# Streaming the feed-forward products' columns from the last to the first

## The chip, the cores and the metric

The kernel runs on one core of one Trainium2 chip. The metric is the device time of one execution in microseconds (us); the kernel before has a median of 1002.88 us over three runs (997.54, 1002.88 and 1003.29). The core's engines are TensorE (PE: matrix products, with PEld for the loads of the stationary operand), VectorE (DVE), ScalarE (ACT), GpSimd (POOL) and SyncE (SP), which issues the transfers here.

## The reference

Attention of two kinds over q, k and v of shape (4, 8, 576, 64): one over means of 4 neighbouring positions (144 of them), repeated 4 times afterwards, and one over a band of less than 4 positions around each query; the two results are added. The sum, as a matrix x of 2304 tokens by 512, goes through two feed-forwards:

```
h = x @ w_in                       # 512 x 2048
x = (h - tanh(h)) @ w_out          # 2048 x 512
gate = sigmoid(x @ w_gate)         # 512 x 1536
out  = (gate * (x @ w_val)) @ w_out2   # 1536 x 512
```

## The kernel before

The tokens are cut into 6 chunks of 384 (`N`), and everything of the feed-forwards is held transposed: 128 features on the partitions, 384 tokens in the free dimension. Each 32-bit number is split into a high part in the format fp32r and a rest (`split`, line 222: ScalarE copies, VectorE subtracts), and each product of two such numbers is made of three matmuls, high by high, high by rest and rest by high. `mm3` (lines 228 to 231) is the one place where they are issued. Its arguments are the output in PSUM, the two parts of the stationary operand, and the two parts of the moving operand.

A matmul has one stationary operand, 128 by 128, which a LDWEIGHTS row loads, and one moving operand, whose columns stream through the array one after the other; each gives one column of the output. There are three callers:

- `h_part` (line 533, called by `h_mm`): hidden features of a chunk. Stationary are the weights, moving is x, 384 columns; four parts of 128 input features accumulate in one bank of PSUM (`ab`). Used by the first feed-forward, and for gate and value of the second.
- `do_y` (line 576): the first feed-forward's second product. Moving is g, 384 columns; 16 blocks of hidden features accumulate in four banks (`acc`).
- `do_out` (line 734): the second feed-forward's second product. Here g is stationary and the weights move, 512 columns; 12 blocks accumulate in three banks at a time (`acc` and `ab`).

The order of the work is written out by hand: the engines' streams are in program order from the second chunk on, and the attention's small products are put between those of the feed-forwards by a counter (`tick`, `work`). The attention's own matmuls (lines 305 to 440) don't go through `mm3`. The results in PSUM are read by ScalarE and VectorE (tanh, sigmoid, copies), which wait by semaphores for the last of the matmuls that write a bank; a framework derives those waits from the tiles and regions that an instruction reads and writes.

Of the kernel before, what the change touches and what calls it, by code (L numbers as in the profile page):

```python
# [53 lines left out]
def tile_kernel(ctx: ExitStack, tc: tile.TileContext, qk, vp, v, w1, w2, mask, ident, out):  # L54
# [3 lines left out]
    def pool(name, bufs, stack=ctx, **kw):  # L58
        return stack.enter_context(tc.tile_pool(name=name, bufs=bufs, **kw))
# [8 lines left out]
    ap = pool("ap", 1, p1)  # L68
# [153 lines left out]
    def split(dst, src):  # L222
# [2 lines left out]
            out=dst[:, 1, :], in0=src, in1=dst[:, 0, :].bitcast(F32), op=ALU.subtract  # L225
        )

    def mm3(o, wh, wl, xh, xl, first, last):
        nc.tensor.matmul(out=o, lhsT=wh, rhs=xh, start=first, stop=False)  # L229
        nc.tensor.matmul(out=o, lhsT=wh, rhs=xl, start=False, stop=False)  # L230
        nc.tensor.matmul(out=o, lhsT=wl, rhs=xh, start=False, stop=last)  # L231
# [304 lines left out]
    def h_part(w, key, bank, k):  # L536
        wh, wl = (w[:, i, k * 128:(k + 1) * 128] for i in range(2))
        x = xt[key, k]
        mm3(bank[:, :N], wh, wl, x[:, 0, :], x[:, 1, :], k == 0, k == KD - 1)
# [34 lines left out]
    def do_y(c, f):  # L574
        g, w = gs.pop((c, f)), weight(1, f, 1)
        if f == 0:
            acc[c] = [acc_bank(e) for e in range(KD)]
        for e in range(KD):
            wh, wl = (w[:, i, e * 128:(e + 1) * 128] for i in range(2))
            mm3(acc[c][e][:, :N], wh, wl, g[:, 0, :], g[:, 1, :], f == 0, f == F1 - 1)  # L580
            if f == F1 - 1:
                defer(1, y_out, c, e)
            if e == 1:
                tick()
        y_done.add((c, f))
        tick()
# [150 lines left out]
    def do_out(i, f, s, g):  # L737
# [3 lines left out]
        for t, bank in enumerate(banks[s]):  # L741
            gh, gl = (g[:, x, t * 128:(t + 1) * 128] for x in range(2))
            mm3(bank, gh, gl, w[:, 0, :], w[:, 1, :], f == 0, f == F2 - 1)
            if f == F2 - 1:
                row = PAIRS[i][s] * N + t * 128
                last = i == len(PAIRS) - 1
                if last:

                    if not ends:
                        ends.extend(p.tile([128, WU], I64, tag="raw", name="ends").bitcast(F32) for p in (rawp, wpools["raw2"]))  # L750
                    at = 3 * s + t
                    o = ends[at // 4][:, at % 4 * DM:at % 4 * DM + DM]
                else:
                    o = xs2.tile([128, DM], F32, tag="o", name="o")
                if last and s == 1 and t == 2:
                    half = DM // 2
                    nc.vector.tensor_copy(out=o[:, :half], in_=bank[:, :half])
                    copy(o[:, half:], bank[:, half:])
                    store(out[row:row + 128, :half], o[:, :half])
                    store(out[row:row + 128, half:], o[:, half:])  # L760
                    continue
                if t % 2:
                    copy(o, bank)
                else:
                    nc.vector.tensor_copy(out=o, in_=bank)
                store(out[row:row + 128, :], o)
            if t == 1:
                tick()
# [91 lines left out]
```

## Time and profile before

| | |
|---|---|
| median of three runs | 1002.88 us (997.54 to 1003.29) |
| span of the profiled execution | 998.4 us; no other time of this execution is listed |
| PE busy | 979.2 us, 98% |
| PEld busy | 914.6 us, 92% |
| VectorE, ScalarE, GpSimd busy | 42%, 37%, 8% |
| share of PE in the chain that ended last | 91% |

The span runs from the first instruction to the last. Matmuls overlap their neighbours, so the mean duration of one is longer than the time it costs; what one costs is the distance from its start to the start of the next.

### The profile page before, as it was taken

How to read it: one execution, taken by the hardware profiler on the slowest of the kernel's cores; microseconds unless marked ns; L12 is line 12 of the kernel's file. 1: busy time of each engine (PE TensorE's matmuls, PEld its weight loads, DVE VectorE, ACT ScalarE, POOL GpSimd, SP SyncE). 2: the span in 40 equal slices, each digit the busy share in tenths (PEclk: the TensorE clock that was granted, in tenths of full speed). 3: DMA queues.
4: the chain of work that ended last, by engine and by line, in shares of the span. 5: the costliest groups of instructions: out<-in, count | busy, mean ns of one | idle time of the engine just before them, and what ended most of it. 6: DMA issues, size and time to landing. Idle time of an engine off the chain costs nothing.

```text
span 998.4 us, 15616 instructions
## 1 busy us (share of the span) xinstructions
PE 979.2 (98%) x6476; PEld 914.6 (92%) x6476; DVE 419.2 (42%) x736; ACT 372.2 (37%) x952; POOL 78.5 (8%) x89
## 2 busy tenths in 40 slices
PE   7889999999999999999999999999999999999998
PEld 7678889999999889999999999999999999999997
DVE  6898864334334343435666553113211114211112
ACT  5867754344344444434456342113111113111111
POOL 2153220300300320000000000000000000000000
PEclk9899999999999999999999999999999999999999
DMA  8566532212203211104444330002000002000001
GB/s 281 165 216 230 177 113 84 62 40 86 61 9 116 63 61 55 60 1 166 159 142 143 127 127 1 9 16 72 32 1 1 3 22 72 32 1 1 1 1 64
DMA packets 33256, 76.63 MB, mean 77 GB/s; under 512 B 3280, under 2 KB 23456, under 8 KB 28832
## 3 DMA queue, kind: packets, MB, share of 16 engines
q1 hardware_dynamic: 33184, 75.62, 23.0%
q8 instruction: 51, 0.84, 0.3%
q14 instruction: 21, 0.17, 0.1%
HBM read 63.02 MB, written 12.58 MB: 76 GB/s over the span
## 4 chain that ended last, share of the span: by engine, by line
PE 91%; DVE 3%; POOL 2%; DMA 2%; ACT 2%; issue 1%; SPq 0%; POOLq 0%; DVEq 0%; ACTq 0%
PE ab L229 18%; PE ab L231 18%; PE ab L230 18%; PE acc L229 10%; PE acc L230 9%; PE acc L231 9%; PE ab L440 2%; PE ab L372 2%; PE ab L305 1%; PE ab L432 1%; PE ab L346 1%; PE ab L334 1%; DMA qk<-in_qk 1%; DVE w L193 1%; PE acc L653 1%
## 5 line engine op out<-in xcount | busy, mean ns | idle before, releaser
L229 PE MATMUL ab<-x,w 128*128 128x384 f32 x952 | 325.5, 342 | 0.3 <-DVE t L242 0.3
L231 PE MATMUL ab<-x,w 128*128 128x384 f32 x952 | 320.4, 337 | 0.0
L230 PE MATMUL ab<-x,w 128*128 128x384 f32 x952 | 320.1, 336 | 0.0
L229 PEld LDWEIGHTS ab<-x,w 128*128 128x128 f32 x952 | 179.2, 188 | 7.6 <-issue 1.8
L230 PEld LDWEIGHTS ab<-x,w 128*128 128x128 f32 x952 | 179.4, 188 | 3.4
L231 PEld LDWEIGHTS ab<-x,w 128*128 128x128 f32 x952 | 179.2, 188 | 0.0
L785 DVE TENSOR_TENSOR p<-ab,p 128x384 f32<-128x384 f32 x72 | 40.2, 558 | 273.4 <-PE ab L231 273.4
L229 PE MATMUL acc<-g,w 128*128 128x384 f32 x384 | 133.2, 349 | 0.0
L230 PE MATMUL acc<-g,w 128*128 128x384 f32 x384 | 129.7, 338 | 0.0
L231 PE MATMUL acc<-g,w 128*128 128x384 f32 x384 | 129.1, 336 | 0.0
L242 DVE TENSOR_TENSOR t<-ab,t 128x384 f32<-128x384 f32 x94 | 52.3, 556 | 153.4 <-ACT t L554 153.4
L781 ACT ACTIVATE p<-ab 128x384 f32<-128x384 f32 x72 | 35.4, 491 | 183.4 <-PE ab L231 183.4
L554 ACT ACTIVATE t<-ab 128x384 f32<-128x384 f32 x94 | 45.9, 488 | 146.3 <-PE ab L231 130.5
L239 ACT ACTIVATE g<-p 128x384 fp32r<-128x384 f32 x72 | 37.8, 524 | 158.0 <-DVE p L785 158.0
L229 PEld LDWEIGHTS acc<-g,w 128*128 128x128 f32 x384 | 72.1, 188 | 2.4 <-issue 1.8
L230 PEld LDWEIGHTS acc<-g,w 128*128 128x128 f32 x384 | 72.3, 188 | 0.7 <-issue 0.6
L231 PEld LDWEIGHTS acc<-g,w 128*128 128x128 f32 x384 | 72.2, 188 | 0.0
L242 DVE TENSOR_TENSOR g<-t,g 128x384 fp32r<-128x384 f32 x96 | 55.9, 583 | 36.6 <-ACT g L239 35.4
L239 ACT ACTIVATE g<-t 128x384 fp32r<-128x384 f32 x96 | 50.3, 524 | 44.7 <-DVE t L242 44.7
L224 DVE TENSOR_TENSOR g<-p,g 128x384 fp32r<-128x384 f32 x72 | 40.2, 559 | 42.6 <-ACT g L239 42.6
L231 PE MATMUL acc<-w,g 128*128 128x512 f32 x144 | 57.1, 396 | 0.0
L230 PE MATMUL acc<-w,g 128*128 128x512 f32 x144 | 57.0, 396 | 0.0
(101 smaller groups left out, 1099.5 us busy)
## 6 DMA issues: line engine op xcount, KB each, us to landing
raw<-in_w SPq DMA_DIRECT2D x34, 1024.0 KB
qk<-in_qk SPq DMA_DIRECT2D x16, 576.0 KB
vr<-in_vp SPq DMA_DIRECT2D x16, 288.0 KB
x<-xo SPq DMA_DIRECT2D x20, 192.0 KB
xs<-x SPq DMA_DIRECT2D x20, 192.0 KB
y<-y SPq DMA_DIRECT2D x20, 192.0 KB
xs<-y SPq DMA_DIRECT2D x20, 192.0 KB
out<-o SPq DMA_DIRECT2D x12, 256.0 KB
```

The costliest lines, as they stand in the source:

```text
L193: nc.vector.tensor_tensor(out=t[:, 1, :], in0=w32, in1=t[:, 0, :].bitcast(F32), op=ALU.subtract)
L224: nc.vector.tensor_tensor(out=dst[:, 1, :], in0=src, in1=dst[:, 0, :].bitcast(F32), op=ALU.subtract)
L229: nc.tensor.matmul(out=o, lhsT=wh, rhs=xh, start=first, stop=False)
L230: nc.tensor.matmul(out=o, lhsT=wh, rhs=xl, start=False, stop=False)
L231: nc.tensor.matmul(out=o, lhsT=wl, rhs=xh, start=False, stop=last)
L239: nc.scalar.activation(out=dst, in_=src, func=ACTF.Copy)
L242: nc.vector.tensor_tensor(out=dst, in0=a, in1=b, op=ALU.subtract)
L372: nc.tensor.matmul(out=sb[r0:r0 + 64, x, :], lhsT=t[r0:r0 + 64, 0, QB * j:QB * j + QB], rhs=t[r0:r0 + 64, 1, w0:w0 + WIN], start=True, sto ...
L440: nc.tensor.matmul(out=ob[r0:r0 + 64, QB * x:QB * x + QB], lhsT=vw[0][:, j - n, i, r0:r0 + 64], rhs=pt[:, x, r0:r0 + 64], start=True, stop ...
L554: nc.scalar.activation(out=t, in_=hb[:, :N], func=ACTF.Tanh)
L781: nc.scalar.activation(out=p, in_=gate[:, :N], func=ACTF.Sigmoid)
L785: nc.vector.tensor_tensor(out=p, in0=val[:, :N], in1=p, op=ALU.mult)
```

## The change

The three matmuls get their output and their moving operand as access patterns that start at the last column and go down by one element. Column j of the input still ends in column j of the output; only the order in which the columns pass is turned. The stationary operand is as before. All calls of `mm3` are affected, no other matmul is.

```
+    def backwards(a):
+        step, n = a.ap[-1]
+        return bass.AP(tensor=a.tensor, offset=a.offset + step * (n - 1), ap=[list(a.ap[0]), [-step, n]])
+
     def mm3(o, wh, wl, xh, xl, first, last):
+        o, xh, xl = backwards(o), backwards(xh), backwards(xl)
         nc.tensor.matmul(out=o, lhsT=wh, rhs=xh, start=first, stop=False)
         nc.tensor.matmul(out=o, lhsT=wh, rhs=xl, start=False, stop=False)
         nc.tensor.matmul(out=o, lhsT=wl, rhs=xh, start=False, stop=last)
```

No instruction is added, removed or moved on any engine: the sequences of PE, VectorE, ScalarE, GpSimd and SyncE are the same but for the line numbers, which grow by 5 behind the new function. What differs is which semaphores some instructions wait for. The rows on PE that name PE's own semaphore grow from 88 to 143; those on VectorE that name PE's shrink from 203 to 146; ScalarE, GpSimd and SyncE wait as before.

On PE, in the second chunk of the first feed-forward, at the change from `do_y` (bank `acc_679`) to the next `do_h` (bank `ab_1845`, the third block of weights). Before:

```order
L229 MATMUL acc_679<-g_1730,w_1693 128x384
L230 MATMUL acc_679<-g_1730,w_1693 128x384
L231 MATMUL acc_679<-g_1730,w_1693 128x384
L229 MATMUL ab_1845<-x_1700,w_591 128x384
L230 MATMUL ab_1845<-x_1700,w_591 128x384
L231 MATMUL ab_1845<-x_1700,w_591 128x384
```

The same place with the change:

```order
L234 MATMUL acc_679<-g_1730,w_1693 128x384
L235 MATMUL acc_679<-g_1730,w_1693 128x384
L236 MATMUL acc_679<-g_1730,w_1693 128x384
L234 MATMUL ab_1845<-x_1700,w_591 128x384 [waits PE_49]
L235 MATMUL ab_1845<-x_1700,w_591 128x384
L236 MATMUL ab_1845<-x_1700,w_591 128x384
```

The first matmul into the bank now names PE's own semaphore; the order is untouched.

On VectorE, in the stretch of the first chunk in which the attention's products alternate with the feed-forward's; `g<-t,g` writes the rest of g behind ScalarE's copy of its high part. Before:

```order
L242 TENSOR_TENSOR t<-ab,t 128x384 [waits Activation_49]
L176 TENSOR_SCALAR raw<-raw 128x1024 [waits DMAHW2_49]
L178 SCALAR_TENSOR_TENSOR raw<-raw 128x1024 [waits DVE_49,Activation_49]
L242 TENSOR_TENSOR g<-t,g 128x384 [waits PE_49,Activation_49]
L416 SCALAR_TENSOR_TENSOR pl<-ab,mask_sb 128x420 [waits PE_49]
```

With the change:

```order
L247 TENSOR_TENSOR t<-ab,t 128x384 [waits Activation_49]
L176 TENSOR_SCALAR raw<-raw 128x1024 [waits DMAHW2_49]
L178 SCALAR_TENSOR_TENSOR raw<-raw 128x1024 [waits DVE_49,Activation_49]
L247 TENSOR_TENSOR g<-t,g 128x384 [waits Activation_49]
L421 SCALAR_TENSOR_TENSOR pl<-ab,mask_sb 128x420 [waits PE_49]
```

The subtraction no longer names PE beside ScalarE; it stands where it stood.

## Rows read from the trace of the kernel before

**Rows 1.** The page: the span, and busy time of each engine.

```profile
span 998.4 us, 15616 instructions
PE 979.2 (98%) x6476; PEld 914.6 (92%) x6476; DVE 419.2 (42%) x736; ACT 372.2 (37%) x952; POOL 78.5 (8%) x89
```

**Rows 2.** The page: the chain that ended last, by engine and by line.

```profile
PE 91%; DVE 3%; POOL 2%; DMA 2%; ACT 2%; issue 1%; SPq 0%; POOLq 0%; DVEq 0%; ACTq 0%
PE ab L229 18%; PE ab L231 18%; PE ab L230 18%; PE acc L229 10%; PE acc L230 9%; PE acc L231 9%; PE ab L440 2%; PE ab L372 2%; PE ab L305 1%; PE ab L432 1%; PE ab L346 1%; PE ab L334 1%; DMA qk<-in_qk 1%; DVE w L193 1%; PE acc L653 1%
```

**Rows 3.** Windows: stretch, length, busy PE, PEld, DVE, ACT, POOL; clock; DMA; GB/s.

```profile
75.00:80.00 5.00, 5.00 (x25) 4.74 (x24) 3.06 (x6) 2.04 (x5) 0.00 (x0) 0.70 0.68 216
400.00:600.00 200.00, 200.00 (x1203) 195.11 (x1203) 108.69 (x164) 93.08 (x166) 0.00 (x0) 1.00 0.33 115
600.00:800.00 200.00, 200.00 (x1056) 187.07 (x1055) 46.08 (x80) 39.08 (x77) 0.00 (x0) 1.00 0.05 17
800.00:990.00 190.00, 190.00 (x1004) 177.78 (x1003) 40.06 (x73) 35.08 (x71) 0.00 (x0) 1.00 0.05 16
```

**Rows 4.** Groups of PE, line 229: shapes, count, busy, mean ns, idle before.

```profile
L229 PE MATMUL ab<-x,w 128*128 128x384 f32 x952 | 325.5, 342 | 0.3 <-DVE t L242 0.3
...
L229 PE MATMUL acc<-g,w 128*128 128x384 f32 x384 | 133.2, 349 | 0.0
...
L229 PE MATMUL acc<-w,g 128*128 128x512 f32 x144 | 56.4, 392 | 0.0
L229 PE MATMUL ab<-w,g 128*128 128x512 f32 x72 | 28.5, 395 | 0.0
...
L229 PE MATMUL acc<-x,w 128*128 128x384 f32 x8 | 3.0, 439 | 0.0
```

**Rows 5.** Timeline of PE, second feed-forward: start us, duration us, instruction.

```profile
801.59 0.39 PE L229 MATMUL acc<-w,g 128*128 128x512 f32 x1
...
803.69 0.34 PE L229 MATMUL ab<-x,w 128*128 128x384 f32 x1
803.86 0.34 PE L230 MATMUL ab<-x,w 128*128 128x384 f32 x1
...
807.85 0.39 PE L229 MATMUL acc<-w,g 128*128 128x512 f32 x1
```

**Rows 6.** Timeline of PE at the low clock, first chunk.

```profile
75.48 0.52 PE L230 MATMUL ab<-x,w 128*128 128x384 f32 x1
75.80 0.52 PE L231 MATMUL ab<-x,w 128*128 128x384 f32 x1
...
76.76 0.52 PE L231 MATMUL ab<-x,w 128*128 128x384 f32 x1
```

**Rows 7.** Groups of PEld, line 229, gate, value and hidden features.

```profile
L229 PEld LDWEIGHTS ab<-x,w 128*128 128x128 f32 x952 | 179.2, 188 | 7.6 <-issue 1.8 <-DVE t L242 0.6 <-DVE ss L291 0.2
```

**Rows 8.** Groups of VectorE: same operations, adjacent elements and every second word.

```profile
L193 DVE TENSOR_TENSOR w<-raw,w 128x1024 fp32r<-128x1024 f32 x34 | 44.0, 1293 | 6.1 <-ACT w L239 6.1
...
L224 DVE TENSOR_TENSOR x<-xs,x 128x384 fp32r<-128x384 f32 x44 | 23.0, 554 | 6.8 <-ACT x L239 6.6
...
L594 DVE COPY y<-acc 128x384 f32<-128x384 f32 x10 | 5.5, 550 | 0.0
...
L765 DVE COPY o<-acc 128x512 f32<-128x512 f32 x6 | 4.1, 688 | 5.5 <-DMA out<-o 5.5
```

**Rows 9.** Timeline of PE: into banks ab_1845 (152.81) and ab_1967 (163.94).

```profile
152.63 0.34 PE L231 MATMUL acc<-g,w 128*128 128x384 f32 x1
152.81 0.34 PE L229 MATMUL ab<-x,w 128*128 128x384 f32 x1
...
163.76 0.34 PE L231 MATMUL acc<-g,w 128*128 128x384 f32 x1
163.94 0.34 PE L229 MATMUL ab<-x,w 128*128 128x384 f32 x1
```

## The prediction

> **What bounds the kernel now.** I read the page's busy times first: PE is busy 979.2 of 998.4 us, VectorE 42%, ScalarE 37% [rows 1]. A busy share alone says little of an engine whose instructions overlap, so the chain of waits came next. It runs over PE for 91% of the span, and the six entries of the three lines of `mm3` make up 82% of it (18, 18, 18, 10, 9 and 9) [rows 2]. The windows then say where that holds: from 400 to 990 us PE has no idle time and the clock is granted in full, while VectorE and ScalarE are busy for half of the time at most (108.69 and 93.08 of 200 us, later 46.08 and 39.08) [rows 3]. So the kernel ends when PE is through its stream, and the price of one matmul of `mm3` decides.
>
> That price is a distance between starts, not the mean of 342 ns in the groups [rows 4]. From the timeline: nine matmuls of 512 columns lie between 801.59 and 803.69, (803.69 - 801.59)/9 = 233.3 ns each; twenty-four of 384 columns lie between 803.69 and 807.85, 4.16/24 = 173.3 ns each [rows 5]. The counts for one of the three lines are 952 + 384 + 8 = 1344 of 384 columns and 144 + 72 = 216 of 512 [rows 4], so 4032 and 648 for all three. 4032 x 0.1733 = 698.9 us and 648 x 0.2333 = 151.2 us, together 850.1 us: 85% of the span goes through the three lines that are changed.
>
> [...]
>
> **The change, part by part.**
>
> *The columns' order.* 4680 matmuls read the moving operand downwards and write the bank downwards. The number of columns, the stationary operand and its loads stay. No row of the trace before shows an access in descending order, so its price is bounded. [...] From above: a column takes two clocks in place of one, the price that the low clock shows, 320 ns for 384 columns and 512/384 x 320 = 426.7 ns for 512 [rows 6]; that is 4032 x 146.7 ns + 648 x 193.3 ns = 591 + 125 = +717 us. Between these ends I take 0, by the nearest rows of another engine that walks memory out of simple order. VectorE subtracts 384 neighbouring elements in 554 ns and 1024 elements of which one input lies in every second word in 1293 ns; that is (1293 - 554)/640 = 1.15 ns per element, against (688 - 550)/128 = 1.08 ns for its copies of neighbouring elements [rows 8]. A step of two words costs there 7% at most. A step of minus one keeps neighbours closer than that: each address is beside the last one, and the set of words is the same as before. It is another engine and another direction, hence the wide bounds.
>
> *The new waits on PE.* 55 more rows on PE name PE's own semaphore. The wait is for work that PE has issued long before, or nothing would be known to be free; but if one had to wait until the matmul before it was out of the array, it would cost the difference of length and distance, 340 - 173 = 167 ns, 55 x 0.167 = 9.2 us in all. The trace has one to look at: the first matmul into `ab_1967` names that semaphore already before the change, and it starts 0.18 us after its predecessor (163.76 to 163.94). The first into `ab_1845` has no such wait before the change, and starts 0.18 us after its own (152.63 to 152.81) [rows 9]. I take 0, and keep 9.2 us as the upper end.
>
> *The waits that VectorE loses.* 57 rows of VectorE no longer name PE. They still wait for ScalarE's copy into the same tile, and VectorE isn't what PE waits for after 400 us [rows 3]. An earlier subtraction gains nothing there. In the first 100 us, where PE does idle, it may shift by fractions of a microsecond. I take 0. If the cover went (PE ahead of VectorE), each subtraction would count with its 0.55 us, but PE would have to become much faster for that.
>
> *Everything else.* ScalarE, GpSimd, SyncE and its transfers have the same instructions, order and waits. The semaphore behind a bank's last matmul comes when its last column is written, whichever column that is, so the readers are released as late as before.
>
> The sum is 998.4 + 0 + 0 + 0 = 998.4 us against the profiled execution's span, which is 4.5 us under the median of 1002.88 and inside the runs' 997.54 to 1003.29. Against the median I forecast **1003 us**: no change.
>
> **The rivals.**
>
> *Two clocks per column (slower).* The bank's write port, or the port that reads the moving operand, handles neighbouring words together only while the addresses rise. Descending columns would then go through one by one, at half the rate. [...] It lies at every one of the 4680 matmuls, each on the path, and costs 717 us in the full case: 1720 us. It decides against my forecast as soon as a matmul of 384 columns costs more than 175.4 ns, for 1% of the time is 10 us, and 10 of the 850 us is 1.2% of 173.3 ns. Against it: pairs of words that lie together upwards lie together downwards too (both lengths are even and the tiles begin with column 0), and VectorE's steps of two words cost little [rows 8]. [...] I give 0.16.
>
> *The excess doubles.* [...] 66.7 us more: 1070 us. [...] 0.10, which stands for all small prices up to that.
>
> *The excess goes (faster).* [...] 0.04.
>
> *The new waits drain the array.* 1012 us, at the edge of 1%. 0.03.
>
> *The pattern is turned back.* Output and input are turned together, so a compiler could write both upwards without changing a result. Nothing would then be different on the chip; this gives 1003 us as well, and I count it with my forecast.
>
> **How the numbers follow.** The forecast, 1003 us, has 0.67; by itself it lies between 993 and 1012 us (the runs' spread of 0.6%, and up to 9.2 us for the waits). With the waits that drain (0.03) and the doubled excess (0.10) the cases from 992 to 1072 us hold 0.80; left out are the half rate (0.16) and the lost excess (0.04). One per cent, 10 us, is what runs of this kernel can tell from no change. Faster by more: 0.04 and 0.01 of the forecast's lower edge, 0.05. Slower by more: 0.16 + 0.10 and half of the drained waits, 0.27. Within: 0.68.
>
> **What would show it.** Right: in the stretch from 400 us on, matmuls of 384 columns still start every 173 ns and those of 512 every 233 ns at the full clock, LDWEIGHTS stays at 188 ns, PE's first matmuls into a bank still follow after 0.17 to 0.18 us, and VectorE's idle time is still put down to PE. Two clocks per column would show as 320 and 427 ns at a granted clock of 1.00, with the span past 1700 us and every other engine's busy time unchanged. [...] Drained waits would show as gaps of up to 0.17 us at the 55 places with all other distances kept. My forecast fails if the distance moves at all in the undisturbed stretch; it would be wrong in its reasoning, though right in its number, if distance and waits moved against each other.

## The result and the profile after

| | before | changed |
|---|---|---|
| median | 1000.71 us, four runs | 1013.75 us, four runs |
| ratio | | 1.0123, 95% interval 1.0096 to 1.0149 |
| profiled execution | span 998.4 us | 1016.59 us, span 1014.8 us |

The changed kernel is slower by 1.2%, 12.3 us of 1000.71 (9.6 to 14.9). The time lies inside the range, but it isn't the forecast of no change: one term of the sum was taken as 0 and is about 13 us.

The page of the changed kernel, span and busy times, answers to [rows 1]:

```profile
span 1014.8 us, 15574 instructions
PE 995.1 (98%) x6476; PEld 929.1 (92%) x6476; DVE 417.5 (41%) x736; ACT 375.7 (37%) x952; POOL 78.2 (8%) x89
```

PE is busy 15.9 us longer, in a span that is 16.4 us longer; VectorE, ScalarE and GpSimd do what they did. The windows show it where PE never waits (stretch, length, busy PE with the number of matmuls, PEld, VectorE, ScalarE, GpSimd, granted clock, DMA share, GB/s); compare [rows 3]:

```profile
600.00:800.00 200.00, 200.00 (x1041) 186.83 (x1040) 49.14 (x83) 41.86 (x78) 0.00 (x0) 1.00 0.07 23
```

At the full clock 1041 matmuls fit into the 200 us that held 1056. The timeline of PE in the second feed-forward (start, duration) says which of them are dearer; it answers to [rows 5]:

```profile
802.84 0.40 PE L234 MATMUL acc<-w,g 128*128 128x512 f32 x1
...
804.94 0.34 PE L234 MATMUL ab<-x,w 128*128 128x384 f32 x1
805.11 0.34 PE L235 MATMUL ab<-x,w 128*128 128x384 f32 x1
805.29 0.34 PE L236 MATMUL ab<-x,w 128*128 128x384 f32 x1
805.46 0.34 PE L234 MATMUL ab<-x,w 128*128 128x384 f32 x1
...
809.18 0.40 PE L234 MATMUL acc<-w,g 128*128 128x512 f32 x1
```

Nine matmuls of 512 columns take 804.94 - 802.84 = 2.10 us, 233.3 ns each, as before. Twenty-four of 384 columns take 4.24 us in place of 4.16: 176.7 ns each in place of 173.3. The single starts lie 0.17 and 0.18 us apart in turn: one matmul has the old distance, the next is some 6.7 ns late. 4032 x 3.33 ns = 13.4 us. Over all matmuls of the rows `ab<-x,w` that start between 600 and 990 us, the mean distance is 176.6 ns against 173.6 before, 3.1 ns more, which makes 12.4 us; the 512-column ones there have 233.7 ns against 232.8, 0.6 us for all 648.

The loads of the stationary operand, which the change leaves alone, take 189 ns against 188 [rows 7]:

```profile
L234 PEld LDWEIGHTS ab<-x,w 128*128 128x128 f32 x952 | 179.6, 189 | 7.7 <-issue 2.0 <-DVE t L247 0.4 <-DVE xo L460 0.2
```

And the first matmul into `ab_1845`, which now names PE's own semaphore, follows as closely as before [rows 9], 0.18 us:

```profile
156.66 0.34 PE L236 MATMUL acc<-g,w 128*128 128x384 f32 x1
156.84 0.34 PE L234 MATMUL ab<-x,w 128*128 128x384 f32 x1
```

The stream accounts for some 13 of the profiled pair's 16.4 us. The other 3 us or so are near what the clock took in that execution. Two windows of the changed kernel:

```profile
30.00:47.00 17.00, 14.21 (x118) 10.34 (x113) 11.48 (x22) 13.56 (x47) 3.05 (x3) 0.70 0.46 151
...
329.00:337.00 8.00, 6.48 (x57) 5.69 (x57) 1.38 (x3) 1.28 (x3) 4.33 (x6) 0.79 0.02 8
```

The same two of the kernel before:

```profile
30.00:47.00 17.00, 14.34 (x135) 10.89 (x134) 13.17 (x25) 15.04 (x50) 2.54 (x3) 0.80 0.51 164
...
329.00:337.00 8.00, 8.00 (x69) 7.02 (x68) 3.80 (x10) 3.65 (x13) 1.81 (x2) 1.00 0.67 186
```

The granted clock is lower by 0.10 over 17 us and by 0.21 over 8 us, 1.7 + 1.7 = 3.4 us of full clock. PE's wait of 1.5 us in the second window doesn't count: the kernel before has it too, 1.8 us long and some 6 us earlier. The other three runs of the changed kernel had mean clocks of 0.992 to 0.997 against 0.990 here, and two of them are at 1009.97 and 1011.8 us; so this part comes and goes between executions.

### The profile page after: what moved, and what is told of

Read it like the earlier page. It is cut to its first block, busy times and chain, and to the rows that moved or that the text cites. A ratio compares the mean times of both kernels' runs of the same rounds, so it can differ in the third digit from the quotient of the medians.

```text
span 1014.8 us, 15574 instructions
## 1 busy us (share of the span) xinstructions
PE 995.1 (98%) x6476; PEld 929.1 (92%) x6476; DVE 417.5 (41%) x736; ACT 375.7 (37%) x952; POOL 78.2 (8%) x89
## 4 chain that ended last, share of the span: by engine, by line
PE 91%; DVE 3%; DMA 2%; ACT 2%; POOL 2%; issue 1%; SPq 0%; POOLq 0%; DVEq 0%; ACTq 0%
PE ab L234 18%; PE ab L235 18%; PE ab L236 18%; PE acc L234 10%; PE acc L235 9%; PE acc L236 9%; PE ab L377 2%; PE ab L445 2%; PE ab L310 1%; PE ab L437 1%; DMA qk<-in_qk 1%; PE ab L351 1%; PE ab L339 1%; PE acc L658 1%; DVE w L193 1%; ACT pl L429 1%
## 5 line engine op out<-in xcount | busy, mean ns | idle before, releaser
L234 PE MATMUL ab<-x,w 128*128 128x384 f32 x952 | 329.7, 346 | 0.1
L235 PE MATMUL ab<-x,w 128*128 128x384 f32 x952 | 324.6, 341 | 0.0
L236 PE MATMUL ab<-x,w 128*128 128x384 f32 x952 | 324.5, 341 | 0.0
L234 PE MATMUL acc<-g,w 128*128 128x384 f32 x384 | 134.5, 352 | 0.0
L235 PE MATMUL acc<-g,w 128*128 128x384 f32 x384 | 131.1, 341 | 0.0
L236 PE MATMUL acc<-g,w 128*128 128x384 f32 x384 | 130.4, 340 | 0.0
```

## Experiments

Theories at the outset: **R**, reading the moving operand downwards costs it; **W**, writing the bank downwards costs it; **S**, the 55 additional waits on PE cost it. Later **D**, the direction by itself, against **P**, the places of the two operands in memory.

**Reading alone.** `mm3` without the reversed output:

```
-        o, xh, xl = backwards(o), backwards(xh), backwards(xl)
+        xh, xl = backwards(xh), backwards(xl)
```

> Only the moving operand is read downwards; the results are written upwards, so that the products come out with their columns in reverse (inside each chunk of 384 tokens, and inside each row of the output). In the changed kernel the starts of 384-column matmuls lie 173.3 and 180.0 ns apart in turn, against 173.3 throughout before; 512 columns stay at 233.3 ns. Theory R (reading downwards costs it): 173.3 and 180.0 in turn again, about 4032/2 x 6.7 ns = 13.4 us, time near 1013 us. Theory W (writing downwards costs it): 173.3 ns throughout, time near 1001 us. Theory S (the 55 additional semaphore waits cost it): this kernel has the 88 waits of before, so 1001 us too, with 173.3 ns.

Measured: 1011.84 us, ratio 1.0097 (1.0071 to 1.0124). Timeline, a step of the second feed-forward:

```profile
805.24 0.40 PE L234 MATMUL acc<-w,g 128*128 128x512 f32 x1
807.34 0.34 PE L234 MATMUL ab<-x,w 128*128 128x384 f32 x1
...
811.58 0.40 PE L234 MATMUL acc<-w,g 128*128 128x512 f32 x1
```

4.24/24 = 176.7 ns for 384 columns, 2.10/9 = 233.3 ns for 512: the distances of the changed kernel, with the waits of the kernel before. R holds. By time it is 9.7 us by the ratio (7.1 to 12.4) and 11.0 us by the medians (1011.84 and 1000.87), somewhat less than the 13 us of the distances. Part of that is the clock: at a mean clock of 0.993 this kernel took 1012.66 and 1012.58 us, the kernel before 1000.54 us, 12.1 us apart. PE waits in the first 100 us for others, and a dearer matmul there may cost nothing, but that was not measured by itself.

**Writing alone.**

```
-        o, xh, xl = backwards(o), backwards(xh), backwards(xl)
+        o = backwards(o)
```

> Only the output in PSUM is written downwards, the moving operand is read upwards; columns come out in reverse. Theory R: 173.3 ns for 384 columns, time near 1001 us. Theory W: 173.3 and 180.0 ns in turn, near 1013 us. Theory S: this kernel has the 143 waits of the changed one, so about 1010 to 1013 us while the distances in the undisturbed stretch stay at 173.3 ns. If reading and writing cost only together (or only against each other), both this and the run with reading alone deviate from R and W in the same way.

Measured: 1001.55 us, ratio 1.0002 (0.9984 to 1.0019).

```profile
802.64 0.39 PE L234 MATMUL acc<-w,g 128*128 128x512 f32 x1
804.74 0.34 PE L234 MATMUL ab<-x,w 128*128 128x384 f32 x1
...
808.90 0.39 PE L234 MATMUL acc<-w,g 128*128 128x512 f32 x1
```

4.16/24 = 173.3 ns: as before. W falls by the distance, and S by the time, since this kernel has the changed kernel's 143 rows with PE's own semaphore (and VectorE's lost waits).

**Only the 512-column matmuls turned.**

```
+        if o.ap[-1][1] != N:
+            o, xh, xl = backwards(o), backwards(xh), backwards(xl)
```

> Reading and writing downwards for the 512-column matmuls alone (648 of 4680); same results as before. R and W both expect 233.3 ns as in the changed kernel and 173.3 ns for 384 columns, time as before, 998 to 1003 us. If the half pause of the 384-column matmuls is something that spreads from the stretch as a whole (a state that reading downwards leaves behind), the 384-column distances show 173.3 and 180.0 in turn here too.

Measured, one run: 999.78 us.

```profile
807.00 0.40 PE L235 MATMUL acc<-w,g 128*128 128x512 f32 x1
809.10 0.34 PE L235 MATMUL ab<-x,w 128*128 128x384 f32 x1
...
813.27 0.40 PE L235 MATMUL acc<-w,g 128*128 128x512 f32 x1
```

2.10/9 = 233.3 ns and 4.17/24 = 173.8 ns. Nothing is left behind for the 384-column matmuls; the whole cost is in those that are turned themselves, and the 512-column ones have next to none here (233.6 ns in mean between 600 and 990 us, 232.8 before).

**Matmuls alone.** 24 in a row of each kind, nothing else running:

```
    for n, rd, wr, cols, kind, at, step in CASES:
        ...
        for i in range(24):
            b = banks[i // 6][:cols, :]
            nc.tensor.matmul(
                out=pattern(b, *way(wr[i % len(wr)], n, at[1], step[1]), n),
                lhsT=w[:, 128 * (i % 4):128 * (i % 4) + cols],
                rhs=pattern(m, *way(rd[i % len(rd)], n, at[0], step[0]), n), start=(i % 6 == 0), stop=(i % 6 == 5),
            )
```

> Matmuls alone, none of the reference's work: 24 in a row of each kind, numbers of columns, directions of reading and writing, first columns, widths of the stationary operand, fp32r and bf16. Up, 384 columns 173.3 ns and 512 columns 233.3 ns as in the kernel. Theory R: 384 columns 176.7 ns on average wherever reading goes down, 173.3 otherwise; theory W the same for writing. If the pauses of 6.7 ns come once per 128 columns after the first (so that the pitch is 60 ns per 128 columns less 6.7 ns), then 256 columns up take 113.3 ns, 448 columns 206.7 ns. If they depend on where in the bank or in the row the stream ends, shifting the first column by 32, 64 or 128 changes the downward average of 176.7 ns. If the loads of the stationary operand cause them, 64 and 32 weight columns in place of 128 take some away. In bf16 nothing is known; 160 and 213.3 ns if the pauses belong to 4-byte reading. Turning the direction from matmul to matmul is between the two directions, 173.3 to 176.7 ns, unless a pause belongs to the jump back to the first column, in which case it is below 173.3 ns.

Rows of the timeline, each a row of merged matmuls of one kind (start, length from the first start to the last end, count). The windows leave out the first few of the 24. In order: fp32r 384 columns read and written up; read up, written down; read down, written up; both down; 512 columns both up; both down; bf16 384 columns up; down:

```profile
29.20 3.63 PE L63 MATMUL b<-xr,ws 128*128 128x384 f32 x20
33.36 3.63 PE L63 MATMUL b<-xr,ws 128*128 128x384 f32 x20
37.35 3.90 PE L63 MATMUL b<-xr,ws 128*128 128x384 f32 x21
41.62 3.90 PE L63 MATMUL b<-xr,ws 128*128 128x384 f32 x21
46.05 4.93 PE L63 MATMUL b<-xr,ws 128*128 128x512 f32 x21
62.56 5.06 PE L63 MATMUL b<-xr,ws 128*128 128x512 f32 x21
182.75 3.41 PE L63 MATMUL b<-xb,wb 128*128 128x384 bf16 x20
186.65 3.42 PE L63 MATMUL b<-xb,wb 128*128 128x384 bf16 x20
```

Less the last one's 0.34 us (0.40 us with 512 columns), (3.63 - 0.34)/19 = 173.2 ns whenever reading goes up, (3.90 - 0.34)/20 = 178.0 ns whenever it goes down: R again, and writing free in both rows. For 512 columns (4.93 - 0.40)/20 = 226.5 against (5.06 - 0.40)/20 = 233.0. In bf16 the direction costs nothing (162.5 ns both ways). In fp32r with 320 columns it costs nothing either; up and down:

```profile
84.20 3.39 PE L63 MATMUL b<-xr,ws 128*128 128x320 f32 x22
87.72 3.39 PE L63 MATMUL b<-xr,ws 128*128 128x320 f32 x22
```

(3.39 - 0.31)/21 = 146.7 ns. What of such a distance doesn't go with the columns can be estimated from the low clock in the trace of before; the window over the 320 ns of [rows 6] (granted clock third from the end):

```profile
75.48:76.76 1.28, 1.28 (x6) 1.28 (x5) 1.28 (x4) 0.00 (x0) 0.00 (x0) 0.50 0.11 35
```

At a granted clock of 0.50 384 columns took 320 ns, so a time that goes with columns and clock alone would be 160 ns at 1.00, or 0.417 ns a column. The distances here grow by as much: 26.5 ns from 320 to 384 columns and 53.3 ns from 384 to 512, 0.41 and 0.42 ns a column. What lies above that, the excess, is in the kernel before 13.3 ns with 384 columns (173.3 - 160) and 20.0 ns with 512 (233.3 - 213.3). Here, upwards, it is 13 ns with 320, 384 and 512 columns alike (146.7 - 133.3 with 320), and 16 ns with 448 (202.7 ns). So where both operands begin at the same place modulo 256 bytes, it doesn't grow with the columns as in the kernel, and the expectation missed with it: 206.7 ns for 448 columns, and 113.3 ns for 256, which took 119.6.

Two things didn't fit D: the kernel before has 233.3 ns for 512 columns upwards, not 226.5, and the changed kernel has 176.7, not 178. Turning the direction from one matmul to the next gave 176.6 to 177.8 ns, no better than upwards throughout; stationary operands of 64 or 32 columns left 173 ns upwards and lowered the downward distance to 175.5.

**Places.** The same loop with starts chosen for both operands, 36 matmuls of each kind; two lines of its list (`S` is the stationary operand's first column, "f" is upwards, "r" downwards):

```
+CASES += [case(384, d, (0,), (S + x,)) for x in (0, 32, 64, 128, 256) for d in "fr"]
+CASES += [case(384, d, (x,)) for x in (16, 32, 48, 64, 96) for d in "fr"]
```

> Matmuls alone again, 36 in a row of each kind, none of the reference's work. Now the places are those of the kernel: moving operand taken in turn from two parts of a tile (high, rest, high), stationary operand from three or four blocks of another. Alone and from one place, 512 columns took 226.7 ns up and 233.3 ns down, while the kernel before shows 233.3 ns up; 384 columns took 173.3 up and 177.8 down, the changed kernel 176.7. Theory D (direction alone): the two-part order gives 233.3 ns for 512 in either direction, 173.3 up and 176.7 down for 384, and shifting the stationary operand by 32 to 256 columns or the moving one by 16 to 96 changes nothing. Theory P (places: the start of a stream against the memory's own divisions, or against the stationary operand): the upward 384 columns get dearer by 2 to 7 ns at starts that are not a multiple of 64 columns (176.2 ns was seen at 32), and for some shift of the second part the 512 columns fall to 226.7 ns; that would be worth 648 x 6.7 ns = 4.3 us in the kernel.

384 columns: both at the same place modulo 64 columns, up, down; the stationary operand shifted by 32, up; the moving one by 16, down; by 32, up:

```profile
149.58 5.36 PE L67 MATMUL b<-xr 128*128 128x384 f32 x30
155.84 5.50 PE L67 MATMUL b<-xr 128*128 128x384 f32 x30
187.51 5.44 PE L67 MATMUL b<-xr 128*128 128x384 f32 x30
244.41 5.46 PE L67 MATMUL b<-xr 128*128 128x384 f32 x30
250.76 5.44 PE L67 MATMUL b<-xr 128*128 128x384 f32 x30
```

Less 0.34 us and over 29: 173.1, 177.9, 175.9, 176.6 and 175.9 ns. Upwards too a stream can be dearer, and moving either operand by 32 columns gives the same. Downwards it doesn't; the stationary operand shifted by 32, then the moving one:

```profile
193.68 5.46 PE L67 MATMUL b<-xr 128*128 128x384 f32 x30
256.75 5.51 PE L67 MATMUL b<-xr 128*128 128x384 f32 x30
```

These are 176.6 and 178.3 ns, against 177.9 at the same place. So the places of both operands count, and the distance between them alone doesn't settle the price. Shifts of the stationary operand by 64, 128 or 256 columns changed nothing. D falls, P stands. The kernel's tiles fit: by the addresses in the built program x and g begin at 32 modulo 256 bytes and nearly all weights at 224, so x lies 64 bytes, 16 columns, on from them; and 16 columns downwards give 176.6 ns, the changed kernel's 176.7. In the 512-column matmuls the weights move and lie 48 columns on from g, a place that the last run of this section has.

**Places in the kernel.** One number of the kernel before, and the same number in the changed kernel, moves x and g against the weights (248 for 32 columns apart, 280 for the same place):

```
-    id_sb = const.tile([128, 232], F32, name="id_sb")[:, :128]
+    id_sb = const.tile([128, 248], F32, name="id_sb")[:, :128]
```

> The kernel before, everything upwards, with one number changed: the tile in front of the left-hand pools is 248 columns wide in place of 232, which moves x and g by 16 columns (64 bytes). Counted modulo 64 columns (256 bytes) x then begins 32 columns away from the weights; in the kernel before it is 16. Theory D (only the direction matters): 173.3 ns for 384 columns and about 1001 us. Theory P (the relation of the two operands' places matters, and the direction changes it): in the measurement alone 384 columns upwards with the two 32 columns apart took 176.1 ns, so 4032 x 2.8 ns = 11 us more, near 1012 us: as much as the change itself costs, with no column turned.

> The kernel before with that tile 280 columns wide: x, g and the weights all begin at the same place modulo 64 columns. Alone this took 173.3 ns for 384 columns and, once settled, 226.7 ns for 512. But the kernel's 512-column matmuls come nine at a time, and the first block of the second feed-forward, whose weights lie that way already, shows 231.3 ns on average and a step of 6.267 us against 6.260 in the other blocks. So both theories expect no change, 1000 to 1002 us.

> The changed kernel (both operands' columns from the last to the first) with the tile 280 columns wide. Theory D: 176.7 ns for 384 columns as in the changed kernel, near 1013 us. Theory P: alone, 384 columns downwards took 177.8 ns with both operands at the same place and 176.7 ns with 16 columns between them, so here 177.8 ns, 4032 x 4.45 = 18 us above the kernel before, near 1019 us.

Measured: 32 columns apart, up: 1005.98 us, ratio 1.0059 (1.0040 to 1.0079). At the same place, up: 1002.82 us, 1.0014 (0.9994 to 1.0033). At the same place, down: 1014.01 us, 1.0137 (1.0098 to 1.0177). The 384-column stretch of the first, and then of the last:

```profile
807.54 0.34 PE L229 MATMUL ab<-x,w 128*128 128x384 f32 x1
...
811.77 0.40 PE L229 MATMUL acc<-w,g 128*128 128x512 f32 x1
```

```profile
807.05 0.34 PE L234 MATMUL ab<-x,w 128*128 128x384 f32 x1
...
811.32 0.40 PE L234 MATMUL acc<-w,g 128*128 128x512 f32 x1
```

4.23/24 = 176.3 ns with every column upwards, 4.27/24 = 177.9 ns at the same place downwards. Both distances are those that P took from the matmuls alone. The times came out lower than P's 1012 and 1019 us, for two reasons. Over all matmuls of the rows `ab<-x,w` between 600 and 990 us the mean distances are 175.8 and 177.8 ns, against 173.6 in the kernel before, so that 9.1 and 17.0 us are to be expected in place of 11 and 18. The other reason is the clock; 68 to 85 us, before and then 32 columns apart:

```profile
68.00:85.00 17.00, 14.30 (x116) 12.40 (x116) 13.55 (x22) 10.75 (x26) 5.56 (x5) 0.80 0.62 201
```

```profile
68.00:85.00 17.00, 14.34 (x135) 12.62 (x132) 16.01 (x26) 12.27 (x29) 6.82 (x6) 1.00 0.73 243
```

The clock doesn't fall there, which gives back 0.20 x 17 = 3.4 us; the profile at the same place downwards has 1.00 in that window too. 9.1 - 3.4 = 5.7 us against 5.9 measured (4.0 to 7.9), 17.0 - 3.4 = 13.6 against 13.7 (9.8 to 17.7). At one mean clock, 0.993, the kernel with 32 columns between took 1010.30 and 1009.91 us and the kernel before 1001.80, 8 us apart.

The shift isn't what decides the clock. The same window in the run with only the 512-column matmuls turned, which has the old tile, and in the run at the same place upwards, which has the widest:

```profile
68.00:85.00 17.00, 14.32 (x133) 12.54 (x132) 16.00 (x26) 12.81 (x30) 6.00 (x5) 1.00 0.71 236
68.00:85.00 17.00, 13.85 (x115) 11.93 (x113) 13.54 (x22) 10.15 (x26) 5.33 (x5) 0.80 0.64 207
```

The first stays at 1.00 without a shift, the second falls to 0.80 with one. What decides it was not found.

**Is there a better place?**

```
+CASES += [case(384, d, (x,)) for x in range(0, 64, 4) for d in "fr"]
```

> Matmuls alone, 36 in a row of each kind, none of the reference's work: the moving operand begins 0, 4, 8, ... 60 columns beyond the stationary one's place modulo 64, upwards and downwards with 384 columns, upwards with 512. Theory P expects upwards between 173.3 (0, 16) and 176.1 ns (32), downwards between 176.1 (48) and 178.3 ns (32), never as cheap as the cheapest upwards. A place at which 384 columns upwards take 166.7 ns (one pause in place of two) would be worth 4032 x 6.7 ns = 27 us in the kernel; I expect none. Theory D expects one value for each direction throughout, which the values at 32 and 48 columns already contradict.

384 columns at the same place up, down; the moving operand shifted by 60 columns up, down; then 512 columns shifted by 48, up:

```profile
26.76 5.36 PE L59 MATMUL b<-xr 128*128 128x384 f32 x30
33.02 5.50 PE L59 MATMUL b<-xr 128*128 128x384 f32 x30
216.76 5.56 PE L59 MATMUL b<-xr 128*128 128x384 f32 x30
223.22 5.46 PE L59 MATMUL b<-xr 128*128 128x384 f32 x30
279.75 7.16 PE L59 MATMUL b<-xr 128*128 128x512 f32 x30
```

173.1, 177.9, 180.0 and 176.6 ns for 384 columns, and (7.16 - 0.40)/29 = 233.1 ns for 512: the 233.3 of the kernel before, whose weights lie 48 columns on from g. With that both things that didn't fit D have their place.

No start gave less than 173.3 ns upwards, so with 384 columns nothing is to be won over the kernel before. With 512 the same place would be better (226.5 ns alone), but the kernel that has it shows 231.2 ns in mean between 600 and 990 us and no gain in time (1.0014). Downwards 384 columns lay between 175.5 and 180.0. The expectation missed the upper end, and downwards both ends: upwards reached 180.0 at 60 columns, dearer than downwards at the same place. Over the shifts by 8 the upward stream was at 173.3 for six of eight, and the downward one never. These are single runs: 48 columns upwards gave 174.6 ns in the run before and 173.3 here, so differences of about 1 ns say nothing.

## Why the prediction was right or wrong

- **The bound: right.** PE's stream sets the end, and 13 us more of it are 12 us more of the time; VectorE's, ScalarE's and GpSimd's busy times moved by 3.5 us at most. (VectorE's 108.69 of 200 us are 54%, a little over the half that the prediction gives as the most; nothing hangs on it.)
- **The columns' order, taken as 0: wrong.** This step failed, by the prediction's own sign: the distance moved in the undisturbed stretch. It costs 3.1 to 3.3 ns for each of the 4032 matmuls with 384 columns and under 1 ns for the 648 with 512, about +13 us. The choice went by VectorE's rows (1.15 against 1.08 ns per element), which say how another engine walks memory; at issue is how TensorE reads the moving operand, of which no row before had anything to show.
- **The waits on PE and those that VectorE loses, 0: right.** The run that only writes downwards has both and the time of before (1.0002). The readers of a bank are released as late as before, too: between 600 and 980 us ScalarE's waiting reads start most often 0.38 us behind the start of the bank's last matmul, VectorE's 0.45 us, in the changed kernel as in the one before.
- **The excess, taken to grow with the columns, by 6.7 ns for each 128 after the first: wrongly read.** The 13.3 and 20.0 ns (estimated above from the low clock; 4032 x 13.3 ns + 648 x 20.0 ns = 66.7 us over the kernel) were taken at two different places: in the kernel the moving operand lies 16 columns on from the stationary one with 384 columns, 48 with 512. Alone and at the same place the excess is 13 ns with 320, 384 and 512 columns. Narrower loads don't remove it (173 ns upwards with stationary operands of 64 or 32 columns); but where the stationary operand lies decides what comes on top: moving it alone by 32 columns made the stream 175.9 ns in place of 173.1. What the stream loses there was not shown.
- **Two clocks per column: didn't happen.** Its place was given as the writing or the reading port. That a column takes one clock is shown by no run, nor a port that handles words in pairs; the 320 ns of its bound were measured at a granted clock of 0.50, and at 1.00 the changed kernel's matmuls of 384 columns lie 176.7 ns apart. Writing downwards is free: the run that does only that has 173.3 ns and the ratio 1.0002. Gaps are another matter: in bf16, 256 columns written to every second word took 215.8 ns, as did 512 to neighbouring ones.
- **The doubled excess: the nearest case.** Its sign was right. No run shows the 66.7 us that it adds; in their place the runs showed 3.3 ns more for a matmul of 384 columns, a quarter of the excess of 13.3 ns, and 12.3 us in all. It had 0.10, and carried the small prices into the range: the forecast by itself ended at 1012 us, so that 1013.75 lies inside through this rival alone. The 0.67 for no change was too much.
- **The excess goes, the pattern is turned back: no.** The distances, 176.7 ns in place of 173.3, show that the columns do run downwards.

What stays open is what the additional 2 to 7 ns are. They came in fp32r (bf16 shows 162.5 and 215.8 ns for 384 and 512 columns in both directions, at the one place measured), with reading, and depend on where the two operands lie modulo 256 bytes; what makes a stream wait was not found.

## What to carry to other kernels

Price a change to a matmul stream by the distance between starts, in a stretch where PE doesn't wait: 3 ns on each of 4032 matmuls is 1.2% of this kernel, and no mean duration or busy share shows it as clearly. A direction that costs nothing to write can cost to read (ratios 1.0002 and 1.0097 here), so turn one of them alone before explaining the pair. A law read off two kinds of matmul, as here that the excess grows with the columns, may come from where their operands lie. And before moving a tile in SBUF in a kernel bound by fp32r matmuls, look at where moving and stationary operands begin modulo 256 bytes: 64 bytes more between them made this one 0.6% slower.

## What the runs showed of the hardware

- Reading the moving operand downwards in fp32r: 175.5 to 180.0 ns for 384 columns, upwards 173.3 to 180.0 ns, by the two operands' places. With 320 columns 146.7 ns either way, in bf16 with 384 columns 162.5 ns either way, each at one place.
- Writing the bank downwards: no cost in fp32r (173.3 ns and the ratio 1.0002 in the kernel, 173.2 ns alone) or bf16 (215.8 ns up and down for 256 columns written to every second word).
- fp32r with 128 and 192 columns: a matmul with its own load every 111.7 ns; 128 columns take no less than 192.
- A stretch of low clock (0.80 in place of 1.00 between 68 and 85 us) is there in some profiles and not in others, with the tiles shifted or not; it is worth 0.20 x 17 = 3.4 us by the clock.
